# Loading a head pair's values onto partitions 32 to 95 in one transfer, and copying the overlaps and memory rows on chip

## Chip, cores, metric

One core of one Trainium2 chip. The metric is device time in microseconds (us). The record marks each run as fast or slow: of the seven runs of before beside runs 1 to 4, the fast ones took 338.6 to 340.5 us and the slow ones 343.93 to 348.09. The medians and ranges below are of all runs, a few slow ones among them; the ratios are of fast runs alone. PE is TensorE, DVE is VectorE, ACT is ScalarE, POOL is GpSimd, SPq is SyncE's queue, which issues most of the loads.

## The reference

Attention in chunks of 32 queries, each with 16 keys to its left, 8 to its right and 8 memory keys; then a Fourier mix over sequence and features, a layer norm and an MLP.

```python
batch, n_heads, seq, head_dim = (4, 8, 768, 64);  n_mem = 8
chunk, left_ctx, right_ctx = (32, 16, 8)
for c in range(seq // chunk):
    k_full = concat([mem_k, k[:, :, max(0, c0 - 16):min(S, c1 + 8)]])     # v_full alike
    a = softmax(scale * q_c @ k_full.T)
    out[:, :, c0:c1] = a @ v_full
x = out as (batch, seq, 512)
u = x + real(fft(fft(x, axis=1), axis=2))
return u + relu(layernorm(u) @ w_ch1) @ w_ch2        # w_ch1: 512 x 2048
```

## The kernel before

Work is cut into 16 head pairs (four per batch). Two chunks of 32 queries share one block of 64 sequence positions, so a block's products need 64 + 16 + 8 value rows and 8 memory rows on 128 partitions. All instructions are put in one fixed order per engine by a small planner (`Plan`), which uses costs written beside each task; on the chip every engine then goes through its list in order (in both traces PE and ACT pass from one line of the kernel to the next in the order of the list: PE 179 times before and 181 in the changed kernel, ACT 126 and 135).

```python
va = [spool.tile([P, NB, 66], FP32) for i in range(6)]           # one per head, two per pair

def e_load_v(n, hh):                                             # three loads per head
    nc.sync.dma_start(v1[16:64, 0:NT, 0:D], ...)                 # 48 rows
    nc.sync.dma_start(v1[0:16, 1:NB, 0:D], ...)                  # the 16 before them
    nc.sync.dma_start(v1[64:72, 0:NT, 0:D], mem_v[...].to_broadcast([NMEM, NT, D]))

def e_overlap(n, hh):                                            # the rows after the block
    nc.gpsimd.tensor_copy(v1[96:128, 0:NT, 0:D + 1], v1[0:32, 1:NB, 0:D + 1])

def e_kT(n):                                                     # keys, blocks 96 apart
    nc.scalar.copy(strided(kTb[n % NKT], 0, [[BS, NB], [8, 8], [1, RB]]), ...)

# ... cut: queries and keys are loaded (2 KB rows), cast (DVE in the first batch, POOL later),
#     turned on PE, copied by ACT; scores on PE, exponentials on ACT; then
def e_values(n, g):        # 24 products xa <- e1, va on PE; needs loads and overlaps
def e_norm(n, g):          # DVE: divides by the sum, writes xsb
# fourier(b): a chain of DVE steps zy, pq, ff, lo (two inputs in SBUF each) with ACT and PE between
# mlp(b): PE products ph and pc, ACT relu; they fill PE wherever it has nothing else
```

The softmax here doesn't subtract the row's maximum and nothing guards it: scores larger than these inputs give would overflow.

Of the kernel before, what the change touches and what calls it, by code (L numbers as in the profile page):

```python
# [16 lines left out]
CHUNK = 32  # L17
# [3 lines left out]
BIGM = 800.0  # L21

# [89 lines left out]
def kernel(  # L112
# [23 lines left out]
    NB = KP // 8  # L136
    BS = 96
# [18 lines left out]
    NV = 6  # L156
    va = [spool.tile([P, NB, 66], FP32, name=f"va{i}") for i in range(NV)]
    NKT = 2
    kTb = [spool.tile([P, NB * BS], BF16, name=f"kTb{i}") for i in range(NKT)]
# [4 lines left out]
    plan = Plan(dict(qf=NS, kf=NS, va=NV // 2, kTb=NKT, qb=1, kb=1, qT=2, tr=1, sc=1, xa=1, e1=3,  # L164
# [6 lines left out]
    mkf = cpool.tile([P, 2, D], FP32)  # L171
    mkb = cpool.tile([P, 2 * D], BF16)
# [11 lines left out]
    ident = cpool.tile([P, P], FP32)  # L184
# [25 lines left out]
    def e_masks():  # L210
        nc.gpsimd.memset(mbias, NEG)
        nc.gpsimd.memset(mbias[0:72, :], 0.0)
        nc.gpsimd.memset(mbias[96:128, 1:2], 0.0)
        nc.gpsimd.affine_select(out=mbias[0:64, 0:1], in_=mbias[0:64, 0:1],
                                compare_op=ALU.is_ge, fill=NEG,
                                base=CHUNK + LEFT + RIGHT - 1, pattern=[[0, 1]],
                                channel_multiplier=-1)
        nc.gpsimd.memset(mbias[0:32, 1:2], NEG)
        nc.gpsimd.affine_select(out=mbias[96:128, 1:2], in_=mbias[96:128, 1:2],
                                compare_op=ALU.is_ge, fill=NEG, base=RIGHT + LEFT - 1,  # L220
                                pattern=[[0, 1]], channel_multiplier=-1)
# [5 lines left out]
    def e_clear_act(t):  # L227
        flat = t if len(t.shape) == 2 else t.rearrange("p a b -> p (a b)")
        nc.scalar.copy(flat, zero[0:flat.shape[0]].to_broadcast(list(flat.shape)))

    def e_ones(i):
        nc.vector.memset(va[i][0:72, :, 64:65], 1.0)
        nc.vector.memset(va[i][0:16, 0, 64:65], 0.0)
        nc.vector.memset(va[i][0:64, NB - 1, 64:65], 0.0)
        nc.vector.memset(va[i][0:16, NB - 1, 64:65], 1.0)

# [12 lines left out]
    def e_load_k(n):  # L249
        b, pr = seq[n]  # L250
        nc.sync.dma_start(kf[n % NS][2:2 + QP],
                          k[b, 2 * pr:2 * pr + 2].rearrange("h (p j) d -> p h (j d)", j=RB))

    def e_load_v(n, hh):
        b, pr = seq[n]
        v1 = va[(2 * n + hh) % NV]
        vb = v[b, 2 * pr + hh]
        nc.sync.dma_start(v1[16:64, 0:NT, 0:D],
                          bass.AP(tensor=vb.tensor, offset=vb.offset,
                                  ap=[[D, 48], [64 * D, NT], [1, D]]))  # L260
        nc.sync.dma_start(v1[0:16, 1:NB, 0:D],  # L261
                          bass.AP(tensor=vb.tensor, offset=vb.offset + 48 * D,
                                  ap=[[D, 16], [64 * D, NT], [1, D]]))
        nc.sync.dma_start(v1[64:72, 0:NT, 0:D],
                          mem_v[b, 2 * pr + hh].unsqueeze(1).to_broadcast([NMEM, NT, D]))

# [13 lines left out]
    def e_overlap(n, hh):  # L280
        v1 = va[(2 * n + hh) % NV]
        nc.gpsimd.tensor_copy(v1[96:128, 0:NT, 0:D + 1], v1[0:32, 1:NB, 0:D + 1])  # L282

# [23 lines left out]
    def e_mkT(n):  # L307
        b, pr = seq[n]
        nc.vector.tensor_copy(
            kTb[n % NKT].rearrange("p (b c) -> p b c", b=NB)[:, 0:NT, 64:72],  # L310
            mkT[:, b * HP + pr, :].unsqueeze(1).to_broadcast([P, NT, NMEM]))

    def e_kT(n):
        nc.scalar.copy(  # L314
            strided(kTb[n % NKT], 0, [[BS, NB], [8, 8], [1, RB]]),
            strided(tr_of.pop((n, 1)), 0, [[8, NB], [1, 8], [KP, RB]]))
# [470 lines left out]
```

## Time and profile before

| | before |
|---|---|
| time, median of the first 3 runs | 342.63 us (341.51 to 344.22) |
| span of the profiled run | 339.3 us |
| busy: PE, DVE, ACT, POOL | 289.6, 183.2, 168.9, 80.6 us |
| 256-byte packets per pair: values, memory rows | 1536, 192 |
| loads per pair | 8 |

How to read it: PE is the engine to keep fed. Its idle time is almost all before 229 us, in the attention and Fourier parts of the four batches; the MLP of the first batch fills holes there, the other three follow it. So the question of any change is what it does to the end of the first batch's MLP: what comes after that takes some 155 to 158 us in every run below. The lines of the profile stand in the prediction.

### The profile page before, as it was taken

Reading aid. Unit: us, or ns where it says so; the run is one execution under the profiler, and the core shown is the slowest. Engines: PE = TensorE matmul, PEld = TensorE weight load, DVE = VectorE, ACT = ScalarE, POOL = GpSimd, SP = SyncE. Lnnn points to the kernel's source line nnn. Section 1 sums busy time; section 2 is a strip of 40 time slices with the busy share of each in tenths; the row PEclk is TensorE's granted clock in tenths of the full one; section 3 lists DMA queues with packets and bytes.
Section 4 is the critical chain, followed back from the end, with each engine's and each line's share of the span. In section 5 each row is a group of like instructions: output and inputs, shape, how many; then the busy total and the mean of one; then the engine's idle time right before and its main releaser. Section 6 shows DMA issues by size and latency. Waiting matters only on the chain.

```text
span 339.3 us, 6789 instructions
## 1 busy us (share of the span) xinstructions
PE 289.6 (85%) x2761; PEld 185.4 (55%) x2761; DVE 183.2 (54%) x356; ACT 168.9 (50%) x297; POOL 80.6 (24%) x89
## 2 busy tenths in 40 slices
PE   0678647969998886969999997898999999999995
PEld 0467536847565565547755654574445454554542
DVE  6964498868089899599773469782010100101001
ACT  7554885557637448676633623335436053250620
POOL 5634594224342637252001200000010000000000
PEclk9999999879999999898999999599999999999999
DMA  7999999999407785692063100000340100201001
GB/s 157 214 183 162 168 229 203 220 173 178 72 3 152 131 182 136 183 201 36 0 110 101 31 3 2 31 31 33 68 119 2 62 31 2 93 0 64 31 32 63
DMA packets 51839, 33.02 MB, mean 97 GB/s; under 512 B 40032, under 2 KB 42080, under 8 KB 51808
## 3 DMA queue, kind: packets, MB, share of 16 engines
q1 hardware_dynamic: 45376, 22.03, 36.9%
q0 software_dynamic: 2688, 4.19, 6.7%
q10 hardware_dynamic: 3744, 6.36, 4.9%
q8 instruction: 22, 0.36, 0.5%
q14 instruction: 9, 0.07, 0.1%
HBM read 28.11 MB, written 6.29 MB: 101 GB/s over the span
## 4 chain that ended last, share of the span: by engine, by line
PE 62%; DVE 14%; DMA 9%; ACT 4%; POOL 3%; issue 3%; SPq 3%; ACTq 0%; POOLq 0%
PE ph L496 23%; PE pc L510 22%; DMA qf<-in_q_dram 8%; PE xa L349 7%; PE pm L445 4%; PE ps L413 2%; SPq L261 2%; DVE zy L373 2%; DVE lo L403 2%; PE sc L325 1%; DVE ff L390 1%; DVE st L457 1%; DVE pq L381 1%; ACT e L333 1%; DVE pq L380 1%
## 5 line engine op out<-in xcount | busy, mean ns | idle before, releaser
L503 ACT ACTIVATE hT<-ph 128x384 f16<-128x384 f32 x128 | 61.2, 492 | 70.5 <-PE ph L496 70.3
L496 PE MATMUL ph<-unT,w_sb 128*128 128x384 f16 x512 | 92.2, 327 | 2.4 <-ACT hT L503 1.8
L510 PE MATMUL pc<-w_sb,hT 128*128 128x512 f16 x384 | 87.3, 382 | 0.0
L516 DVE SCALAR_TENSOR_TENSOR osb<-pc,rstd,xsb 128x512 f32<-128x512 f32 x24 | 17.8, 746 | 98.3 <-PE pc L510 98.3
L496 PEld LDWEIGHTS <-w_sb 128*128 128x128 f16 x512 | 48.3, 97 | 37.9 <-issue 8.2
L510 PEld LDWEIGHTS <-hT 128*128 128x128 f16 x384 | 37.2, 98 | 42.4 <-issue 1.5
L282 POOL COPY va<-va 32x780 f32<-32x780 f32 x32 | 36.2, 1138 | 50.0 <-DMA va<-in_v_dram 37.9
L333 ACT ACTIVATE e<-sc,mbias 128x384 f32<-128x384 f32 x64 | 33.7, 579 | 20.0 <-PE sc L325 19.1
L349 PE MATMUL xa<-va,e 128*64 128x65 f32 x768 | 35.4, 253 | 8.6 <-ACT e L333 3.7
L349 PEld LDWEIGHTS xa<-va,e 128*64 128x64 f32 x768 | 30.6, 162 | 15.7 <-issue 7.7
L463 ACT ACTIVATE un<-xsb,mu_s 128x512 f16<-128x512 f32 x24 | 17.3, 722 | 24.5 <-DVE mu_s L458 15.8
L359 DVE RECIPROCAL zs<-xa 128x6 f32<-128x6 f32 x32 | 6.1, 190 | 34.5 <-PE xa L349 34.3
L325 PE MATMUL sc<-qT,kTb 64*128 64x64 bf16 x384 | 12.8, 207 | 12.6 <-ACT kTb L314 11.0
L484 POOL TENSOR_SCALAR rstd<-mu_s 128x6 f32<-128x6 f32 x4 | 1.0, 244 | 89.7 <-DVE osb L516 83.7
L413 PE MATMUL ps<-cosS,lo 128*128 128x193 f16 (+1 forms) x72 | 16.6, 285 | 4.6 <-DVE lo L403 4.5
L274 POOL CAST qb<-qf 96x1024 bf16<-96x1024 f32 x12 | 14.9, 1242 | 20.8 <-DMA qf<-in_q_dram 11.9
L413 PE MATMUL ps<-cosS,hi 128*128 128x193 f16 (+1 forms) x72 | 16.7, 285 | 3.4 <-DVE ff L390 3.2
L425 ACT CAST up<-ps 128x386 f16<-128x386 f32 x16 | 9.7, 605 | 19.4 <-PE ps L413 17.8
L325 PEld LDWEIGHTS <-kTb 64*128 64x128 bf16 x384 | 8.8, 104 | 18.5 <-ACT kTb L314 12.3
L360 DVE TENSOR_TENSOR xsb<-xa,zs 128x384 f32<-128x384 f32 x32 | 17.8, 557 | 1.1
L398 ACT CAST hi<-ff 128x768 f16<-128x768 f32 x16 | 13.2, 832 | 10.1 <-DVE ff L390 9.9
L403 DVE TENSOR_TENSOR lo<-ff,hi 128x768 f16<-128x768 f32 x16 | 16.8, 1063 | 2.2 <-ACT hi L398 2.1
(90 smaller groups left out, 356.2 us busy)
## 6 DMA issues: line engine op xcount, KB each, us to landing
qf<-in_q_dram SPq DMA_DIRECT2D x16, 384.0 KB
kf<-in_k_dram SPq DMA_DIRECT2D x16, 384.0 KB
out_dram<-osb ACTq DMA_DIRECT2D x24, 256.0 KB, 2.0
va<-in_v_dram SPq DMA_DIRECT2D x32, 144.0 KB, 5.8
w_sb<-in_moe_w_ch_dram POOLq DMA_DIRECT2D x8, 512.0 KB, 16.1
va<-in_v_dram SPq DMA_DIRECT2D x32, 48.0 KB, 6.8
va<-in_mem_v_dram SPq DMA_DIRECT2D x32, 24.0 KB
unT<-un SPq DMA_TRANSPOSE x18, 2.4
```

The costliest lines, as they stand in the source:

```text
L282: nc.gpsimd.tensor_copy(v1[96:128, 0:NT, 0:D + 1], v1[0:32, 1:NB, 0:D + 1])
L325: nc.tensor.matmul(sc[:, hh, t6, :], kT[r0:r0 + 64, t * BS:t * BS + P], qT[r0:r0 + 64, ts(t, 64)], start=True, stop=True, tile_position=(r ...
L333: nc.scalar.activation(e1[:, :, :, ts(half, 32)], sc[:, :, 0:6, ts(half, 32)], AFT.Exp, bias=mbias[:, half:half + 1], scale=1.0 / math.sqr ...
L349: nc.tensor.matmul(xa[64 * half:64 * half + 64, st, hh, 0:65], e1[:, hh, t6, :], v1[:, 6 * g + t6, 0:65], start=True, stop=True)
L360: nc.vector.tensor_tensor(xs[b][:, 3 * g:3 * g + 3, 2 * pr * D:(2 * pr + 2) * D] .rearrange("p s (h d) -> p s h d", h=2), xa[:, :, :, 0:D] ...
L403: nc.vector.tensor_tensor(lo[:, ab].rearrange(fl), ff_of[b, par][:, ab].rearrange(fl), hi[:, ab].rearrange(fl), ALU.subtract)
L413: nc.tensor.matmul(out_[:, sp, :], part[:, ab, sp * 3 + st, c0:c1], tab[:, sp, st, :], start=(st == 0 and i == 0), stop=(st == 2 and i == 1))
L463: nc.scalar.activation(un, xs[b][:, kt, :], AFT.Identity, bias=mu_of[b][:, kt, 0:1], scale=-1.0)
L496: nc.tensor.matmul(ph[:, 0:384], w1_sb[:, dt, ts(ht, P)], unT_of[b][:, dt, sh * 384:(sh + 1) * 384], start=(dt == 0), stop=(dt == NDT - 1))
L503: nc.scalar.activation(hT_of[b, sh][:, ht, :], ph_of.pop((b, sh, ht))[:, 0:384], AFT.Relu, bias=0.0, scale=-1.0)
L510: nc.tensor.matmul(pc_of[b, sh, stl], hT_of[b, sh][:, ht, ts(stl, P)], w2_sb[:, ht, :], start=(ht == 0), stop=(ht == NHT - 1))
L516: nc.vector.scalar_tensor_tensor(osb, pc_of.pop((b, sh, stl)), rstd_of[b][:, st:st + 1], xs[b][:, st, :], ALU.mult, ALU.add)
```

## The change

Intent: the value loads are many 256-byte packets to few partitions. Bring the 64 rows of a block onto partitions 32 to 95 in one transfer for both heads, and make the rest (left overlap, right overlap, twelve-fold memory rows) by copies on chip, so that fewer loads and packets are needed. Cut to its core:

```diff
-    va = [spool.tile([P, NB, 66], FP32, name=f"va{i}") for i in range(6)]
+    va = [spool.tile([P, 2, NT, 66], FP32, name=f"va{i}") for i in range(3)]
+    mv = [spool.tile([NMEM, 2, D], FP32, name=f"mv{i}") for i in range(3)]
-    kTb = [spool.tile([P, NB * BS], BF16, name=f"kTb{i}") for i in range(NKT)]
+    kTb = [spool.tile([P, NT, P], BF16, name=f"kTb{i}") for i in range(NKT)]
@@ loads: six per pair become two
+        nc.sync.dma_start(mv[n % NV], mem_v[b, 2 * pr:2 * pr + 2].rearrange("h m d -> m h d"))
+        nc.sync.dma_start(v1[PAD:PAD + 64].rearrange("p h t c -> p (h t) c")[:, :, 0:D],
+                          vb.rearrange("h (t p) d -> p (h t) d", p=64))
@@ copies
-        nc.gpsimd.tensor_copy(v1[96:128, 0:NT, 0:D + 1], v1[0:32, 1:NB, 0:D + 1])     # per head
+        if side == 0:                                                              # per pair
+            nc.gpsimd.tensor_copy(v1[0:32, :, 1:NT, 0:D + 1], v1[64:96, :, 0:NT - 1, 0:D + 1])
+        else:
+            nc.gpsimd.tensor_copy(v1[96:128, :, 0:NT - 1, 0:D + 1], v1[32:64, :, 1:NT, 0:D + 1])
+    def e_memv(n, eng):                            # DVE in the first batch, POOL in the others
+        eng.tensor_copy(va[n % NV][0:NMEM, :, :, 0:D],
+                        mv[n % NV].unsqueeze(2).to_broadcast([NMEM, 2, NT, D]))
@@ keys: 13 groups of 8 instead of 8, blocks 128 apart
-            strided(kTb[n % NKT], 0, [[BS, NB], [8, 8], [1, RB]]),
+            strided(kTb[n % NKT], PAD - 8 * KOFF, [[P, NT], [8, 13], [1, RB]]),
@@ planner's costs
-        lv = [add("SP", 1.1, ..., moved=2.3) for hh in range(2)]
+        lv = add("SP", 0.8, lambda: e_load_v(n), ..., take=("va",), moved=2.0)
-        ov = [add("POOL", 0.84, lambda hh=hh: e_overlap(n, hh), [lv[hh]]) for hh in range(2)]
+        ov = [add("POOL", 1.55, lambda side=side: e_overlap(n, side), [lv]) for side in range(2)]
+        ov.append(add(cn, 1.0 if first else 1.7, lambda: e_memv(n, ce), [ov[0]]))
```

Left out: the masks for the new places, cleared and set buffers, three constants moved into other buffers.

More of the change, by code (lines that the diff above doesn't have):

```diff
@@ L21 @@
 BIGM = 800.0
+PAD = 32
+KOFF = 3
 def rev_ap(src, last, count, outer=()):
@@ L135 @@
     KP = QP + 8
-    NB = KP // 8
-    BS = 96
     HS = S // 2
@@ L155 @@
     kf = [spool.tile([KP, 2, RB * D], FP32, name=f"kf{i}") for i in range(NS)]
-    NV = 6
-    va = [spool.tile([P, NB, 66], FP32, name=f"va{i}") for i in range(NV)]
+    NV = 3
+    va = [spool.tile([P, 2, NT, 66], FP32, name=f"va{i}") for i in range(NV)]
+    mv = [spool.tile([NMEM, 2, D], FP32, name=f"mv{i}") for i in range(NV)]
     NKT = 2
-    kTb = [spool.tile([P, NB * BS], BF16, name=f"kTb{i}") for i in range(NKT)]
+    kTb = [spool.tile([P, NT, P], BF16, name=f"kTb{i}") for i in range(NKT)]
     HP = H // 2
     seq = [(b, pr) for b in range(B) for pr in (0, 2, 1, 3)]
-    plan = Plan(dict(qf=NS, kf=NS, va=NV // 2, kTb=NKT, qb=1, kb=1, qT=2, tr=1, sc=1, xa=1, e1=3,
+    plan = Plan(dict(qf=NS, kf=NS, va=NV, kTb=NKT, qb=1, kb=1, qT=2, tr=1, sc=1, xa=1, e1=3,
                      xsb=3, fold=2, hl=1, up=4, dn=4, acc=2, mlp=2, un=3, unT=2, hT=1, osb=3))
@@ L170 @@
     NPR = B * H // 2
-    mkf = cpool.tile([P, 2, D], FP32)
-    mkb = cpool.tile([P, 2 * D], BF16)
+    mkf = fpool.tile([P, 2, D], FP32, tag="osb", bufs=3, name="mkf")
+    mkb = fpool.tile([P, 2 * D], BF16, tag="osb", bufs=3, name="mkb")
     mkT = cpool.tile([P, NPR, NMEM], BF16)
@@ L183 @@
     zero = cpool.tile([P, 1], FP32)
-    ident = cpool.tile([P, P], FP32)
+    ident = fpool.tile([P, P], FP32, tag="osb", bufs=3, name="ident")
     ident_h = cpool.tile([P, P], FP16)
@@ L210, in e_masks @@
     def e_masks():
-        nc.gpsimd.memset(mbias, NEG)
-        nc.gpsimd.memset(mbias[0:72, :], 0.0)
-        nc.gpsimd.memset(mbias[96:128, 1:2], 0.0)
-        nc.gpsimd.affine_select(out=mbias[0:64, 0:1], in_=mbias[0:64, 0:1],
-                                compare_op=ALU.is_ge, fill=NEG,
-                                base=CHUNK + LEFT + RIGHT - 1, pattern=[[0, 1]],
-                                channel_multiplier=-1)
-        nc.gpsimd.memset(mbias[0:32, 1:2], NEG)
-        nc.gpsimd.affine_select(out=mbias[96:128, 1:2], in_=mbias[96:128, 1:2],
-                                compare_op=ALU.is_ge, fill=NEG, base=RIGHT + LEFT - 1,
-                                pattern=[[0, 1]], channel_multiplier=-1)
+        nc.gpsimd.memset(mbias, 0.0)
+        for half in range(2):
+            first, last = PAD - LEFT + CHUNK * half, PAD + CHUNK * (half + 1) + RIGHT - 1
+            nc.gpsimd.affine_select(out=mbias[:, half:half + 1], in_=mbias[:, half:half + 1],
+                                    compare_op=ALU.is_ge, fill=NEG, base=last,
+                                    pattern=[[0, 1]], channel_multiplier=-1)
+            nc.gpsimd.affine_select(out=mbias[:, half:half + 1], in_=mbias[:, half:half + 1],
+                                    compare_op=ALU.is_ge, fill=NEG, base=-first,
+                                    pattern=[[0, 1]], channel_multiplier=1)
+        nc.gpsimd.memset(mbias[0:NMEM, :], 0.0)
     def e_scales():
@@ L227, in e_clear_act @@
     def e_clear_act(t):
-        flat = t if len(t.shape) == 2 else t.rearrange("p a b -> p (a b)")
+        flat = t.rearrange("p a b -> p (a b)" if len(t.shape) == 3 else "p a b c -> p (a b c)")
         nc.scalar.copy(flat, zero[0:flat.shape[0]].to_broadcast(list(flat.shape)))
     def e_ones(i):
-        nc.vector.memset(va[i][0:72, :, 64:65], 1.0)
-        nc.vector.memset(va[i][0:16, 0, 64:65], 0.0)
-        nc.vector.memset(va[i][0:64, NB - 1, 64:65], 0.0)
-        nc.vector.memset(va[i][0:16, NB - 1, 64:65], 1.0)
+        nc.vector.memset(va[i][0:NMEM, :, :, D:D + 1], 1.0)
+        nc.vector.memset(va[i][32:64, :, :, D:D + 1], 1.0)
+        nc.vector.memset(va[i][64:96, :, :, D:D + 1], 1.0)
     def e_mkf():
@@ L250, in e_load_k, with e_load_v @@
         b, pr = seq[n]
-        nc.sync.dma_start(kf[n % NS][2:2 + QP],
+        nc.sync.dma_start(kf[n % NS][KOFF:KOFF + QP],
                           k[b, 2 * pr:2 * pr + 2].rearrange("h (p j) d -> p h (j d)", j=RB))
-    def e_load_v(n, hh):
+    def e_load_v(n):
         b, pr = seq[n]
-        v1 = va[(2 * n + hh) % NV]
-        vb = v[b, 2 * pr + hh]
-        nc.sync.dma_start(v1[16:64, 0:NT, 0:D],
-                          bass.AP(tensor=vb.tensor, offset=vb.offset,
-                                  ap=[[D, 48], [64 * D, NT], [1, D]]))
-        nc.sync.dma_start(v1[0:16, 1:NB, 0:D],
-                          bass.AP(tensor=vb.tensor, offset=vb.offset + 48 * D,
-                                  ap=[[D, 16], [64 * D, NT], [1, D]]))
-        nc.sync.dma_start(v1[64:72, 0:NT, 0:D],
-                          mem_v[b, 2 * pr + hh].unsqueeze(1).to_broadcast([NMEM, NT, D]))
+        v1 = va[n % NV]
+        vb = v[b, 2 * pr:2 * pr + 2]
+        nc.sync.dma_start(mv[n % NV], mem_v[b, 2 * pr:2 * pr + 2].rearrange("h m d -> m h d"))
+        nc.sync.dma_start(v1[PAD:PAD + 64].rearrange("p h t c -> p (h t) c")[:, :, 0:D],
+                          vb.rearrange("h (t p) d -> p (h t) d", p=64))
     qT_of, kT_of, qb_of, kb_of, tr_of, e1_of, sc_of, xa_of, xs = ({} for _ in range(9))
@@ L278, in e_cast_k, with e_overlap @@
         eng.tensor_copy(kb_of[n].rearrange(cp_b), kf[n % NS].rearrange(cp_q, j=RB))
-    def e_overlap(n, hh):
-        v1 = va[(2 * n + hh) % NV]
-        nc.gpsimd.tensor_copy(v1[96:128, 0:NT, 0:D + 1], v1[0:32, 1:NB, 0:D + 1])
+    def e_overlap(n, side):
+        v1 = va[n % NV]
+        if side == 0:
[5 more added lines that the diff above has]
+                        mv[n % NV].unsqueeze(2).to_broadcast([NMEM, 2, NT, D]))
     def e_turn_q(n):
@@ L309, in e_mkT @@
         nc.vector.tensor_copy(
-            kTb[n % NKT].rearrange("p (b c) -> p b c", b=NB)[:, 0:NT, 64:72],
+            kTb[n % NKT][:, :, 0:NMEM],
             mkT[:, b * HP + pr, :].unsqueeze(1).to_broadcast([P, NT, NMEM]))
@@ L314, in e_kT @@
         nc.scalar.copy(
-            strided(kTb[n % NKT], 0, [[BS, NB], [8, 8], [1, RB]]),
-            strided(tr_of.pop((n, 1)), 0, [[8, NB], [1, 8], [KP, RB]]))
+            strided(kTb[n % NKT], PAD - 8 * KOFF, [[P, NT], [8, 13], [1, RB]]),
+            strided(tr_of.pop((n, 1)), 0, [[8, NT], [1, 13], [KP, RB]]))
     def e_scores(n, g):
@@ L324, in e_scores @@
                 r0 = 64 * hh
-                nc.tensor.matmul(sc[:, hh, t6, :], kT[r0:r0 + 64, t * BS:t * BS + P],
+                nc.tensor.matmul(sc[:, hh, t6, :], kT[r0:r0 + 64, t, :],
                                  qT[r0:r0 + 64, ts(t, 64)], start=True, stop=True,
@@ L345, in e_values @@
             for hh in range(2):
-                v1 = va[(2 * n + hh) % NV]
+                v1 = va[n % NV]
                 for half in range(2):
@@ L349, in e_values @@
                     nc.tensor.matmul(xa[64 * half:64 * half + 64, st, hh, 0:65],
-                                     e1[:, hh, t6, :], v1[:, 6 * g + t6, 0:65],
+                                     e1[:, hh, t6, :], v1[:, hh, 6 * g + t6, 0:65],
                                      start=True, stop=True)
@@ L528 @@
     t_id = add("POOL", 0.5, lambda: make_identity(nc, ident))
-    t_clear["va", 0] = add("ACT", 1.0, lambda: e_clear_act(va[0]), [t_zero])
-    t_clear["va", 1] = add("POOL", 0.9, lambda: nc.gpsimd.memset(va[1], 0.0))
+    t_clear["va", 0] = add("ACT", 1.8, lambda: e_clear_act(va[0]), [t_zero])
     t_scales = add("DVE", 0.2, e_scales, [t_iota])
@@ L535 @@
         t_clear["kf", i] = add("ACT", 1.15, lambda i=i: e_clear_act(kf[i]), [t_zero])
-        for m in (2 * i, 2 * i + 1):
-            t_clear["va", m] = add("ACT", 1.0, lambda m=m: e_clear_act(va[m]), [t_zero])
+        t_clear["va", i] = add("ACT", 1.8, lambda i=i: e_clear_act(va[i]), [t_zero])
     for i in range(NKT):
@@ L572, in attention @@
                  take=("kf",), moved=1.3)
-        lv = [add("SP", 1.1, lambda hh=hh: e_load_v(n, hh),
-                  [t_ones[2 * n + hh] if 2 * n < NV else None],
-                  take=("va",) if hh == 0 else (), moved=2.3) for hh in range(2)]
+        lv = add("SP", 0.8, lambda: e_load_v(n), [t_ones[n] if n < NV else None],
+                 take=("va",), moved=2.0)
         first = b == 0
@@ L586, in attention @@
                  take=("kTb",))
-        ek = add("ACT", 0.85, lambda: e_kT(n), [tk, mk], give=(ktag,))
+        ek = add("ACT", 1.15, lambda: e_kT(n), [tk, mk], give=(ktag,))
         for g in range(2):
```

## The prediction

> **What bounds the kernel now.** I read the page first (busy shares and slices), then busy time by stretches of 10 us, then the chain of work that ended last, the waits (those of the transfer queue too), the groups, and last the transfer packets that the trace records.
>
> ```profile
> PE 289.6 (85%) x2761; PEld 185.4 (55%) x2761; DVE 183.2 (54%) x356; ACT 168.9 (50%) x297; POOL 80.6 (24%) x89
> PE   0678647969998886969999997898999999999995
> DVE  6964498868089899599773469782010100101001
> DMA  7999999999407785692063100000340100201001
> ```
>
> TensorE works 289.6 of 339.3 us; 49.7 us are idle. From 229 us on it does nothing but the two MLP products and is full: no change to the loads can shorten that. The transfers are full in the first nine slices, about 76 us, and then loosen.
>
> ```profile
> 40.00:50.00 10.00, 2.77 (x30) 2.30 (x31) 9.86 (x20) 8.77 (x14) 9.84 (x11) 1.00 1.12 205
> 70.00:80.00 10.00, 7.28 (x88) 5.61 (x89) 6.71 (x18) 5.09 (x10) 2.07 (x2) 0.83 1.09 166
> 90.00:100.00 10.00, 10.00 (x113) 5.71 (x111) 5.44 (x7) 4.67 (x8) 3.74 (x3) 1.00 0.01 2
> 110.00:120.00 10.00, 6.91 (x88) 4.68 (x88) 8.55 (x13) 5.11 (x8) 6.75 (x6) 1.00 0.81 133
> 140.00:150.00 10.00, 7.71 (x113) 4.91 (x112) 8.89 (x14) 7.82 (x15) 3.94 (x5) 1.00 1.00 178
> ```
>
> The columns are the stretch, then busy us of PE, weight loads, DVE, ACT, POOL, then clock, transfer share and GB/s. From all such rows the idle time of PE is: 0 to 40 us 15.9; 40 to 80 us 12.5; 80 to 100 us 0.2; 100 to 160 us 11.0; 160 to 210 us 0.9; after that 9.9, of which some 5 are the tail. From 90 to 100 us nothing is loaded at all.
>
> ```profile
> 32.79 7.19 DMA qf<-in_q_dram
> 40.10 1.03 POOL qb L274
> ...
> 48.45 7.04 SPq L261
> ...
> 57.05 14.37 DMA qf<-in_q_dram
> 71.54 1.04 POOL qb L274
> 72.63 0.66 PE trq L288 x8
> ...
> 100.89 3.01 DMA out_dram<-osb
> 104.28 0.34 SPq L264
> 104.71 4.47 DMA qf<-in_q_dram
> ```
>
> The chain runs through the loads three times: query loads that stand 7 and 14 us in full queues, and at 104 us the loading queue, which has just waited for a store of the output. Head pairs of the second batch are thus finished late: their last value products start at 92.1 and 94.3 us, and the second batch's Fourier work on DVE begins only then (zy at 96 us). DVE is busy 9.8 of 20 us from 80 to 100 us: waiting, not bound.
>
> ```profile
> SPq L261 <- DMA out_dram<-osb: 20.0, 2, 19.5
> SPq L251 <- DMA kf<-in_k_dram: 7.4, 8, 1.1
> ```
>
> The second line, with the landing times in the trace, shows a rule of this program: a load starts only when the load issued eight earlier on it has landed (35.97 then 36.05 us, 43.21 then 43.27, 75.62 then 75.64). A pair has eight loads, so about one pair is on its way at a time. The first line is the same rule caught on an output store: 19.5 us without a load, just before 104 us.
>
> [...] 256-byte packets take 18 ns while the first pair is alone (some 360 land per 0.5 us), but 38 to 50 ns later, and then 170 to 260 land per 0.5 us. [...] the POOL overlap copy takes 827 ns at best and 1138 on average, DVE's small kTb copy 174 at best and 391 on average. [...] 24 value products take 1.57 us before 45 us and 0.85 later.
>
> **The change, part by part.**
>
> ```profile
> L282 POOL COPY va<-va 32x780 f32<-32x780 f32 x32 | 36.2, 1138 | 50.0 <-DMA va<-in_v_dram 37.9
> L274 POOL CAST qb<-qf 96x1024 bf16<-96x1024 f32 x12 | 14.9, 1242 | 20.8 <-DMA qf<-in_q_dram 11.9
> L314 ACT COPY kTb<-trk 128x832 bf16<-128x832 bf16 x16 | 13.7, 854 | 5.6 <-PE trk L304 4.6 <-POOL va L282 0.9
> ```
>
> Loads. A pair moves 384 packets of 2 KB (query, key), 1536 of 256 B (values) and 192 of 256 B (memory rows, twelve-fold); after it, 384, 1536 and 16. While full, pairs follow each other every 7 us (query landings near 8.5, 15, 21.5, 29.5). The 2 KB packets land at about 65 per 0.5 us: 384 / 65 x 0.5 = 2.95 us. The rest, about 4 us, is values. If all value packets run as in the undisturbed stretch, 1536 / 360 x 0.5 = 2.1 us. Estimate after: 2.95 + 2.1 + 0.3 = 5.4 us per pair, 1.6 less; eight pairs are loaded in the full stretch, so 13 us of transfer time go. With four loads per pair the rule of eight spans two pairs, so the 19.5 us wait is likely to shrink or go.
>
> POOL. The overlap is two copies of 32 x (2 x 11 x 65 = 1430) instead of two of 32 x 780: 834 ns (the median) x 1430 / 780 = 1.53 us alone, x 1138 / 834 = 2.09 us disturbed. The memory copy (8 x 1536) at 1.07 ns per element is 1.64 us, disturbed as the cast is (1242 / 1033) 1.97 us. A pair of batches two to four costs 2 x 2.09 + 1.97 + 1.24 + 1.08 = 8.5 us on POOL, now 2 x 1.14 + 2.32 = 4.6. In all 80.6 + 32 x 0.95 + 12 x 1.97 - 0.8 = 134 us. Twelve pairs need 102 us of the 165 between 33 and 198 us: it lies beside other work, but a batch takes 34 us and can't follow faster.
>
> ACT. The key copy grows from 832 to 1248 elements. From 800 ns at 768 and 854 at 832 the slope is 0.84 ns: 1.2 us, 16 x 0.35 = 5.6 us more; in the first batch it lies on the chain (11.0 and 19.2 us), so about 1 us there.
>
> DVE. Four memory copies in the first batch: the 1024-element cast takes 0.68, so 1.0 us each, 4 us, in a batch where DVE still makes tables; perhaps 0.5 us on the path. Summed over minimum, locks cost DVE some 20 us now; POOL's extra 53 us of a present 80 might add 10, and perhaps 2 on the path, since its Fourier chain is broken by other waits.
>
> PE does the same products. The score product's keys begin at 128-element steps instead of 96, which should change nothing. The moved constants and smaller count of memsets are worth less than 1 us.
>
> **Where it lands.** The first batch (to 38 us) [...] about 6.5 us per pair; faster loads don't help, and the first pair's overlap takes two longer copies: +1.5 us with the key copy. From 40 to 80 us the wait for the query at 71.5 us (2.8 us of idle PE) should go, and about 1 of the 50 to 60 us stretch: -3.5. The second batch's attention should end near 76 us, limited by POOL, instead of 95, so DVE starts its Fourier part up to 19 us sooner, and TensorE still has the first MLP (42 us) to fill with. Of 11.0 us of idle from 100 to 160 us I take 7 back. With it the last 3.6 us hole (210 to 220 us) shrinks by 1 to 2. Locks and longer POOL latency give 2 back. Sum: 1.5 - 3.5 - 7 - 1.5 + 2 = -8.5, and I take another 2 for work of the last pair that moves into idle time before 80 us: -10.5 us, 342.6 to 332.
>
> **Rivals.** A: the loads shrink but TensorE hides it: idle before 160 us is of DVE's making (DVE is 8.6 to 10 busy in most of 100 to 160 us), so only the 3.5 us come back and the first batch costs 1.5: about 340. For it: after 95 us the chain is full of DVE. Against it: DVE was half idle just before. B: POOL becomes the pace. At 8.5 us per pair, overlaps come after the point that the fixed order of the other engines assumes, and TensorE, in order, stands before value products; PE would lose 5 to 10 us, time 340 to 350. For it: POOL work on copies grows by half as much again as all POOL does now. Against it: it had 76% idle. C: everything falls into place and PE is full from 77 us on: 240 us of work left, less 3.5 done earlier, plus 8 of holes and tail: span 322, time 325.
>
> **Range and chances.** My sum sits between C (one in four) and A (three in ten), with B one in ten. So 332, range 323 to 341. Two per cent is 335.8: faster 0.6, within 0.34, slower 0.06.
>
> **What would show it.** Right: about four loads per pair, value packets at about 18 to 25 ns, transfers no longer full to 76 us, no PE wait for the query near 71 us, the second batch's last value products before 82 us, zy of it before 84 us, PE idle from 100 to 160 us under 6 us. Wrong: value packets still at 40 ns; value products or exponentials waiting for the overlap or memory copies; a new long wait of the load queue on an output store; DVE operations stretched by over 15 us in sum; POOL over 150 us.

## The result

358.78 us, median of 4 runs (354.18 to 359.25), against 342.59 of before (341.51 to 344.22): ratio 1.0438, 95% interval 1.0343 to 1.0534. The change is slower. (A ratio here and below is the mean time of one kernel's fast runs over that of the other's fast runs of the same rounds, so not the ratio of the medians quoted. The two differ most in runs 1 to 4: four of the seven runs of before in that job were slow, its median is 343.93, its fast runs took 338.6 to 340.5.)

The page of the changed kernel, busy time and slices as shown of before:

```profile
PE 291.1 (81%) x2761; PEld 185.5 (52%) x2761; DVE 215.9 (60%) x345; ACT 173.7 (49%) x295; POOL 127.1 (36%) x100
PE   1556836689928588947899999598999999999995
DVE  6999299898799969799883357978010010201001
DMA  6982899943935009790004310010051010100101
```

PE does the same work (291.1 us) in a longer span: some 17 us more are idle. The transfers are no longer full throughout the first 76 us (two of the first eight slices are well below, six are still at 8 or 9 tenths). The packets themselves are faster, as foreseen: those of a pair's values took 18 to 25 ns on average in the first 36 us, where before they took 23 in the first pair and 37 to 44 in those after it, and up to 570 of them landed per 0.5 us (292 GB/s; a pair's 1536 value packets landed in 1.72 us, 228 GB/s). But DVE is busy 32.7 us longer, and 47 us more went to POOL. Stretches of 10 us; the columns are PE, weight loads, DVE, ACT, POOL, clock, transfer share, GB/s:

```profile
100.00:110.00 10.00, 3.07 (x35) 2.51 (x34) 9.93 (x9) 4.11 (x6) 9.76 (x7) 0.71 0.16 38
120.00:130.00 10.00, 4.94 (x31) 3.06 (x29) 9.08 (x11) 3.04 (x4) 5.41 (x3) 0.74 0.01 2
160.00:170.00 10.00, 6.72 (x40) 4.71 (x39) 10.00 (x10) 4.63 (x8) 7.53 (x4) 0.54 0.23 41
```

In these DVE is full, PE is a third to two thirds busy, and little is loaded. In the first row DVE gets through nine instructions in 10 us. Four of DVE's instructions there, with three of POOL's, from the instructions in order of time (start, length, both in us):

```profile
97.50 1.67 DVE L380 TENSOR_TENSOR pq<-zy 128x768 f32<-128x768 f32 x1
98.43 1.98 POOL L276 COPY va<-va 32x1430 f32<-32x1430 f32 x1
99.10 2.12 DVE L381 TENSOR_TENSOR pq<-zy 128x768 f32<-128x768 f32 x1
100.47 1.99 POOL L278 COPY va<-va 32x1430 f32<-32x1430 f32 x1
101.26 1.24 DVE L389 COPY ff<-pq 128x6 f32<-128x6 f32 x1
...
102.52 2.14 POOL L281 COPY va<-mv 8x1536 f32<-8x1536 f32 x1
103.26 2.42 DVE L389 COPY ff<-pq 128x6 f32<-128x6 f32 x1
```

The two engines take turns. The `pq` at 97.50 waits until POOL's cast ends (98.36) and then runs its own 0.8 us or so; POOL's copy at 98.43 waits until that `pq` ends (99.17) and then runs its own 1.2 us; the next `pq` waits for it, and so on. (Each is some 0.13 us shorter than alone, 0.81 against 0.95 and 1.24 against 1.37; records of neighbours on one engine overlap here by up to 0.11 us.) A `pq` alone takes 0.95 us, the copy of six elements 0.15: here 2.12 and 2.42. That last copy ends (105.68) only when two of POOL's instructions have ended, the copy at 102.52 (104.66) and a cast after it (105.65). By groups (count, then busy us and mean ns of one), first two of before, then the changed kernel:

```profile
L373 DVE TENSOR_TENSOR zy<-xsb 128x768 f32<-128x768 f32 x16 | 16.3, 1021 | 0.2
L403 DVE TENSOR_TENSOR lo<-ff,hi 128x768 f16<-128x768 f32 x16 | 16.8, 1063 | 2.2 <-ACT hi L398 2.1
```

```profile
L276 POOL COPY va<-va 32x1430 f32<-32x1430 f32 x16 | 31.2, 1952 | 23.5 <-DMA va<-in_v_dram 14.3
L281 POOL COPY va<-mv 8x1536 f32<-8x1536 f32 x12 | 22.0, 1833 | 0.6
L373 DVE TENSOR_TENSOR zy<-xsb 128x768 f32<-128x768 f32 x16 | 24.1, 1515 | 0.2
L403 DVE TENSOR_TENSOR lo<-ff,hi 128x768 f16<-128x768 f32 x16 | 21.9, 1374 | 0.1
L314 ACT COPY kTb<-trk 128x1248 bf16<-128x1248 bf16 x16 | 19.2, 1202 | 0.8 <-PE trk L304 0.8
```

I call the **stretch** of DVE the sum, over all its instructions in the trace, of the time above the shortest of the same line and operation. It was 21.4 us before and is 51.4 now. (The prediction's "locks" are this sum. Records of neighbours overlap a little, so it is a measure, not a share of the span. It does not put the runs below in their order: run 15 has 41.0 and is slower than the changed kernel.)

Where on the way it was lost, in us from the start, from the first and last instruction of each part in the traces:

| | before | changed |
|---|---|---|
| first batch's values done | 39.9 | 44.4 |
| first batch's Fourier part done (last `st`) | 80.7 | 82.3 |
| first product of the MLP | 76.6 | 80.7 |
| second batch's values done | 95.2 | 94.2 |
| second batch's Fourier part, length from second `zy` to last `st` | 35.4 | 46.5 |
| third batch's, likewise | 32.7 | 38.5 |
| fourth batch's (POOL has nothing to copy then) | 30.7 | 30.3 |
| first batch's MLP done | 181.4 | 199.8 |
| end | 339.3 | 357.4 |

All 18 us are lost before the first batch's MLP is done, and the two Fourier parts that run beside POOL's copies are 11.1 and 5.8 us longer, the one that doesn't is not.

### The profile page after: what moved, and what is told of

Same layout as the page of the kernel before. It is cut to its first block, busy times and chain, and to the rows that moved or that the text cites. A ratio compares the mean times of both kernels' runs of the same rounds, so it can differ in the third digit from the quotient of the medians.

```text
span 357.4 us, 6684 instructions
## 1 busy us (share of the span) xinstructions
PE 291.1 (81%) x2761; PEld 185.5 (52%) x2761; DVE 215.9 (60%) x345; ACT 173.7 (49%) x295; POOL 127.1 (36%) x100
## 4 chain that ended last, share of the span: by engine, by line
PE 60%; DVE 31%; ACT 5%; issue 3%; ACTq 0%; DVEq 0%
PE ph L496 22%; PE pc L510 22%; PE xa L349 6%; PE ps L413 5%; DVE zy L373 4%; PE pm L445 4%; DVE lo L403 3%; DVE ff L390 3%; DVE pq L381 3%; DVE pq L380 2%; DVE st L457 2%; DVE ff L389 2%; DVE xsb L451 2%; ACT e L333 1%; DVE va L281 1%
## 5 line engine op out<-in xcount | busy, mean ns | idle before, releaser
L276 POOL COPY va<-va 32x1430 f32<-32x1430 f32 x16 | 31.2, 1952 | 23.5 <-DMA va<-in_v_dram 14.3
L278 POOL COPY va<-va 32x1430 f32<-32x1430 f32 x16 | 26.9, 1679 | 0.9
L373 DVE TENSOR_TENSOR zy<-xsb 128x768 f32<-128x768 f32 x16 | 24.1, 1515 | 0.2
L398 ACT CAST hi<-ff 128x768 f16<-128x768 f32 x16 | 13.4, 837 | 20.0 <-DVE ff L390 19.8
L281 POOL COPY va<-mv 8x1536 f32<-8x1536 f32 x12 | 22.0, 1833 | 0.6
L403 DVE TENSOR_TENSOR lo<-ff,hi 128x768 f16<-128x768 f32 x16 | 21.9, 1374 | 0.1
L413 PE MATMUL ps<-cosS,hi 128*128 128x193 f16 (+1 forms) x72 | 17.8, 298 | 4.8 <-DVE ff L390 3.2
L413 PE MATMUL ps<-cosS,lo 128*128 128x193 f16 (+1 forms) x72 | 17.6, 297 | 4.5 <-DVE lo L403 4.5
L413 PEld LDWEIGHTS <-lo 128*128 128x128 f16 (+1 forms) x120 | 13.8, 115 | 11.9 <-DVE lo L403 11.1
L314 ACT COPY kTb<-trk 128x1248 bf16<-128x1248 bf16 x16 | 19.2, 1202 | 0.8 <-PE trk L304 0.8
## 6 DMA issues: line engine op xcount, KB each, us to landing
w_sb<-in_moe_w_ch_dram POOLq DMA_DIRECT2D x8, 512.0 KB, 14.3
```

The source lines that it names most:

```text
L276: nc.gpsimd.tensor_copy(v1[0:32, :, 1:NT, 0:D + 1], v1[64:96, :, 0:NT - 1, 0:D + 1])
L278: nc.gpsimd.tensor_copy(v1[96:128, :, 0:NT - 1, 0:D + 1], v1[32:64, :, 1:NT, 0:D + 1])
L281: eng.tensor_copy(va[n % NV][0:NMEM, :, :, 0:D], mv[n % NV].unsqueeze(2).to_broadcast([NMEM, 2, NT, D]))
L314: nc.scalar.copy(strided(kTb[n % NKT], PAD - 8 * KOFF, [[P, NT], [8, 13], [1, RB]]), strided(tr_of.pop((n, 1)), 0, [[8, NT], [1, 13], [KP, ...
L373: nc.vector.tensor_tensor(zy_of[b, par][:, :, c0:c0 + P], xb[:, :, c0:c0 + P], xb[:, :, HD + c0:HD + c0 + P], ALU.add if par == 0 else ALU ...
L403: nc.vector.tensor_tensor(lo[:, ab].rearrange(fl), ff_of[b, par][:, ab].rearrange(fl), hi[:, ab].rearrange(fl), ALU.subtract)
```

## The experiments

Three theories. **P**: POOL's reading copies and DVE's operations with two inputs in SBUF exclude each other, and the longer copies stretch the Fourier chain. **O**: the new costs gave the planner a worse order. **L**: POOL's sheer length makes values late. For the gain that did not come there is also **D**: the faster loads were hidden anyway. (The "rival D" in the expectations of 2, 8 and 13 is another: small transfers fill the queues again.) I write "before" for the median of that kernel in the same job.

### 1. POOL writes as long, but reads nothing

```diff
-            nc.gpsimd.tensor_copy(v1[0:32, :, 1:NT, 0:D + 1], v1[64:96, :, 0:NT - 1, 0:D + 1])
+            nc.gpsimd.memset(v1[64:96, :, 1:NT, 0:D + 1], 0.001)
-            nc.gpsimd.tensor_copy(v1[96:128, :, 0:NT - 1, 0:D + 1], v1[32:64, :, 1:NT, 0:D + 1])
+            nc.gpsimd.memset(v1[32:64, :, 1:NT, 0:D + 1], 0.001)
@@ memory rows on POOL
+            eng.memset(va[n % NV][0:NMEM, :, :, 0:D], 0.001)
```

> The changed kernel with its POOL copies (both overlaps, the memory rows of batches two to four) replaced by memsets of the same shapes on POOL, in the same places and the same order; wrong results on purpose. POOL then works as long as before on va (about 1.4 us each) but reads nothing. Theory P (POOL's reads and DVE's two-input operations exclude each other): DVE's stretching (time over each group's minimum, summed) falls from 51 us to 25 or less, and the time from 358.8 to 345 or less. Rival O (the fixed order, computed with the new costs, is worse) and rival L (POOL's sheer length makes the values late): DVE may shorten, but the time stays above 352.

Measured: 341.48 us (338.41 to 343.97), before 343.93, ratio 1.0081 (0.991 to 1.0253). The result is wrong on purpose. The stretch is 29.2 us, above the 25 that I had set. The same places and waits in the order, and 17 us are gone against the 358.78 of the changed kernel (another job; the fast runs, 338.4 to 343.2 and 354.2 to 359.3, don't touch). Two things in the edit besides: the memsets write the copies' source rows, so most values are one constant, and a constant exponent (`mhalf`) was changed with them. Run 6 below has random data.

```profile
L276 POOL MEMSET va<- 32x1430 f32 x16 | 22.5, 1409 | 30.8 <-DMA va<-in_v_dram 25.7 <-PE ph L499 4.6
L278 POOL MEMSET va<- 32x1430 f32 x16 | 21.8, 1365 | 0.7
L384 DVE TENSOR_TENSOR pq<-zy 128x768 f32<-128x768 f32 x8 | 7.6, 950 | 0.0
L312 DVE COPY kTb<-mkT 128x96 bf16<-128x96 bf16 x16 | 8.3, 519 | 0.4 <-PE sc L328 0.3
```

The memsets are stretched little (1409 and 1365 ns on average, 1282 at best, 3.3 us in all; the copies in their places 1952 and 1679, 1367 at best, 14.3 us in all), and `pq` is back at 950 ns on average. The small one-input copy into `kTb` still takes 519 ns, 177 at best. So P holds, with a remainder: POOL is 22 us less busy than in the changed kernel, and 341 is not the 332 of run 5, which has no copies.

### 2. All rows by transfer

```diff
-        nc.sync.dma_start(mv[n % NV], mem_v[...])
+        # per head: v1[16:32, hh, 1:NT], v1[96:104, hh, 0:NT-1] from v, v1[0:8, hh, :] from mem_v
     (no overlap and no memory copies; the planner's costs as in the changed kernel)
```

> The changed kernel with both overlaps and the memory rows loaded again by transfers (six small ones per pair beside the large one onto partitions 32 to 95), no copy on chip, order unchanged. Theory P: DVE's stretching falls to about 15 us, below the kernel before (21), and the time to 335 to 343. Rival O: above 352. Rival D (the transfers were the point: 720 more packets of 256 B per pair fill them again): transfers full to 76 us again, 345 or more.

Measured: 348.03 us (345.22 to 351.37), before 343.93, ratio 1.0222 (1.004 to 1.0404); the result is right. Stretch 12.4 us, as theory P asked, but the time did not follow all the way, as rival D said: the transfers are full again, a pair now takes nine loads, and the first batch's values end at 50.5 us. It is still 11 us faster than the changed kernel; the small transfers cost 16 against run 5, which has neither them nor copies.

### 3. The kernel before in the order of the change

```diff
-        lv = [add("SP", 1.1, ..., moved=2.3) for hh in range(2)]
+        lv = add("SP", 0.8, lambda: (e_load_v(n, 0), e_load_v(n, 1)), ..., moved=2.0)
-        ov = [add("POOL", 0.84, ...
+        ov = [add("POOL", 1.55, ...
+        ov.append(add(cn, 1.0 if first else 1.7, lambda: None, [ov[0]]))
```

> The kernel before, its instructions unchanged, but ordered by the costs that the change gives its planner (values of a pair as one task, memory copy as a task that issues nothing). Rival O: 350 or more. Theory P: the order matters little, 338 to 347.

Measured: 342.52 us (339.27 to 343.68), before 343.93, ratio 1.0072 (0.9945 to 1.0199). The new costs alone do no harm to the kernel before. And runs 1 and 5 keep the changed kernel's own order and take 341 and 332 us, so theory O falls for this change. (How much order can weigh in this kernel otherwise, see 14.)

### 4 and 6. The kernel before with as much more POOL work

```diff
         nc.gpsimd.tensor_copy(v1[96:128, 0:NT, 0:D + 1], v1[0:32, 1:NB, 0:D + 1])
+        for _ in range(3 if hh == 1 and n >= HP else 1):
+            nc.gpsimd.tensor_copy(v1[96:128, 0:NT, 0:D + 1], v1[0:32, 1:NB, 0:D + 1])   # 4
+            nc.gpsimd.memset(v1[96:128, 0:NT, 0:D + 1], 0.001)                          # 6 instead
```

> The kernel before with its overlap copy done twice per head, and four times for the second head of each pair of batches two to four: 56 more copies of 834 ns, 47 us of POOL work, as the change adds; nothing else changed, the result stays right. Theory P: DVE's stretching rises from 21 to 40 us or more and the time to 349 or more. Rival O: under 345.

> As the run with 56 more POOL copies in the kernel before (353 us), but the 56 added instructions are memsets of the same shape on the same rows, which write and don't read; wrong results on purpose. Theory P (reads exclude DVE's two-input operations): most of the 10 us go, 342 to 347. If POOL's sheer time, or its writes, make the loss: 350 or more.

Measured: with copies 353.33 us (352.97 to 355.76), before 343.93, ratio 1.0421 (1.0327 to 1.0515), result right. With memsets 342.18 us (339.52 to 344.18), before 344.0, ratio 0.9986 (0.9886 to 1.0086), wrong on purpose. The added instructions, first with copies, then with memsets:

```profile
L284 POOL COPY va<-va 32x780 f32<-32x780 f32 x56 | 58.7, 1048 | 3.5
151.69 4.45 POOL L284 COPY va<-va 32x780 f32<-32x780 f32 x3
153.87 1.58 DVE L383 TENSOR_TENSOR pq<-zy 128x768 f32<-128x768 f32 x1
```

```profile
L284 POOL MEMSET va<- 32x780 f32 x56 | 43.2, 771 | 3.3
142.85 2.35 POOL L284 MEMSET va<- 32x780 f32 x3
143.53 0.95 DVE L383 TENSOR_TENSOR pq<-zy 128x768 f32<-128x768 f32 x1
```

The last two lines of each are three added instructions in a row, with a `pq` that starts while they run: beside copies both are stretched, beside memsets neither. It is so throughout the two traces (counted where one had at least 0.3 us left when the other began). Of `zy`, `pq`, `ff` and `lo` with two inputs, 13 began while a POOL copy ran, and all 13 were lengthened by about the rest of that copy; 22 copies began while one of them ran, and all 22 were lengthened likewise. With memsets, 3 and 15 met in this way: none was lengthened by more than 17 ns. In run 1, with memsets too, 13 of 15 and 8 of 8 went unhindered; the other two waited on into a cast that followed the memset. DVE's small one-input copies did wait for memsets (4 of 5 here, 8 of 8 in run 1).

43 us of memsets between the overlap and the value products that wait for them cost nothing; copies in the same places cost the 4% that the change cost. That is P against L (a memset is a little shorter, 742 ns against 829 at best, 5 us in all), in a kernel with none of the change's other parts. The stretch rose only to 30.5 us with copies (I had said 40) and to 26.9 with memsets: it is a rough guide, and the time moved by more than it. Part of the loss with copies is thus probably the same lock on its other side: POOL's own lengthening (20.5 us with copies, 7.7 with memsets, over the shortest of each), which makes values late. I did not part the two.

### 5. No copies at all

```diff
     def e_overlap(n, side): ...
+        return
     def e_memv(n, eng): ...
+        return
```

> The changed kernel with neither the overlap copies nor the memory copies, all else in its place and order; wrong results on purpose (overlap and memory rows stay zero). It is the most that the faster loads could give. If my prediction's sum for the loads (-12 us) was right and only the copies spoiled it: 325 to 333. If the loads were hidden (rival A of the prediction): 337 to 343.

Measured: 332.12 us (330.08 to 332.38), before 344.0, ratio 0.9677 (0.959 to 0.9764); wrong on purpose, the data stay random. The first batch's values end at 41.7 us, its Fourier part at 75.6, the second's at 122.0, the first MLP at 174.1. So the copies on chip cost 27 us (359 against 332): 80 us of POOL's time (127.1 busy against 46.9), and four copies on DVE. The 12 us below the kernel before are not the loads' alone, as that kernel has 36 us of overlap copies, which are gone here too. Run 13 below has no copies either, and transfers at least as full as before, and is 6 us below before already: some 5 us are left for the faster loads, no more than two plans can differ by. D is not refuted.

### 7. Memory rows by transfer

```diff
+            nc.sync.dma_start(v1[0:NMEM, hh, :, 0:D], mem_v[...].to_broadcast([NMEM, NT, D]))
     def e_memv(n, eng): ...
+        return
```

> The changed kernel with its memory rows loaded twelve-fold by two transfers per pair again, the overlap copies kept on POOL, order unchanged. By POOL time the memory copies are 22 of the 47 us that POOL gained, and the 4 on DVE go too; if the loss of 16 us goes by time: 349 to 353. Rival: the loss comes from the overlaps of the first batch and the long copies, 354 or more.

Measured: 352.05 us (350.05 to 352.78), before 344.0, ratio 1.027 (1.0191 to 1.0348). The result was wrong, and that was not meant: the left overlap's copy writes partitions 0 to 31 and comes after the load, so it covers the memory rows. The overlap copies are the same, so I let the time stand: without the memory copies 7 us of the loss are gone, less what the two loads cost, and the larger rest is left with the overlaps.

### 8, 11 and 12. Left overlap by transfer, and who copies the rest

```diff
+            nc.sync.dma_start(v1[16:32, hh, 1:NT, 0:D], ...)          # 8, 11, 12: left overlap
+            nc.sync.dma_start(v1[0:8, hh, :, 0:D], mem_v[...])        # 8, 12: memory rows
-        ov = [... e_overlap(n, side) for side in range(2)]
+        ov = [add("POOL", 1.7, lambda: e_overlap(n, 1), [lv])]        # 12: "ACT", 1.4
+        # 11: e_memv on ACT
```

> A candidate: the large transfer onto partitions 32 to 95, the left overlap (16 rows) and the memory rows by small transfers, only the right overlap copied on POOL (one copy of 1.5 us per pair, less than the 1.67 of before), planned anew with these costs. Theory P: DVE's stretching at 20 us or less; [...] 334 to 342. Rival D (the small transfers fill the queues again): 343 to 350.

> Candidate: large transfer, left overlap by two small transfers per pair, right overlap on POOL (1.5 us per pair), memory rows on ACT. Beside the candidate with memory rows loaded (341.5) it has 192 packets of 256 B less per pair and 23 us more on ACT: 335 to 341.

> Candidate: as the one with left overlap and memory rows loaded (341.5 us), but the right overlap copied by ACT, so POOL copies nothing of va. Theory P: DVE's stretching falls from 24 us to 15 or less and the time to 333 to 339. Rival (its transfers are the bound): 340 or more.

Measured, all with right results: 341.53 us (339.34 to 342.05), ratio 0.996 (0.9883 to 1.0036); 364.77 us (363.1 to 365.6), ratio 1.0682 (1.0584 to 1.0781); 349.09 us (347.66 to 350.32), ratio 1.0214 (1.0128 to 1.03). The first came out at the edge of what was foreseen, level with before (stretch 23.7 us, not 20). The two with ACT missed my figures by 24 and 10 us or more. In 12 the stretch did fall, to 13.9 us, and the time rose all the same: 22 us of copies on ACT cost 8 us more than the same copies on POOL in 8. In 11 the memory rows' copies on ACT cost 23 us more than their transfers in 8, at about the same stretch (25.1 us). So there are losses in this kernel that a stretched DVE does not explain; each of these runs has its own plan too.

### 9 and 10. Copies on ACT

```diff
-            nc.gpsimd.tensor_copy(v1[0:32, ...
+            nc.scalar.copy(v1[0:32, ...                               # 9: both overlaps
-        eng.tensor_copy(va[n % NV][0:NMEM, ...
+        nc.scalar.copy(va[n % NV][0:NMEM, ...                         # 9 and 10: memory rows
```

> The changed kernel with all three copies (both overlaps, memory rows) on ACT, planned anew; the result stays right. ACT takes an estimated 1.35 us for 1430 elements and 1.45 for 1536 (slope 0.84 ns per element, from its copies of 768 and 832), 16 x 4.15 = 66 us more on an engine busy 174. [...] it lands near the run without copies (332): 332 to 340. Rival: ACT becomes the pace of the attention (about 8.5 us per pair), 343 or more.

> The changed kernel with the memory rows alone copied by ACT (16 x 1.45 us), overlaps on POOL; the result stays right. It repeats, with a right result, the run that loaded them (352): 346 to 353. If the memory copies were most of the loss: under 343.

Measured, both right: 382.36 us (377.92 to 383.64), ratio 1.1146 (1.1007 to 1.1284), and 368.84 us (367.44 to 371.86), ratio 1.0805 (1.07 to 1.091). For the first the rival holds: DVE's stretch is down to 14.2 us, but ACT is busy 240.7 us (173.7) and value products wait for exponentials (54.2 us in all, 29 times). The 332 to 340 supposed that what DVE and POOL wait for each other is the whole loss. For the second, the waits of the profile show (second and third line) two of the ways in which one slow engine stops another:

```profile
POOL va L276 <- DMA va<-in_v_dram: 36.7, 11, 11.9
ACT va L281 <- POOL va L276: 7.8, 2, 7.3
PE sc L325 <- ACT kTb L314: 10.0, 1, 10.0
```

ACT's memory copy stands in its list behind POOL's overlap, and what ACT does next (keys, exponentials) waits with it. Why it comes to 369, I did not follow to the end.

### 13, 14 and 16. Overlaps inside the large transfer, no copy

A transfer of 96 partitions (8 to 103) per head brings a block's rows and both overlaps at once for ten of twelve blocks; the first and last block, which have no neighbour, come in two small ones.

```diff
+        for hh in range(2):
+            nc.sync.dma_start(v1[8:104, hh, 1:NT - 1, 0:D],
+                              bass.AP(..., offset=vb.offset + (hh * S + 64 + 8 - PAD) * D,
+                                      ap=[[D, 96], [64 * D, NT - 2], [1, D]]))
+        for t, lo, hi in ((0, 32, 112), (NT - 1, 16, 96)):
+            nc.sync.dma_start(v1[lo:hi, :, t, 0:D], ...)
+        # memory rows: two loads; no e_overlap, no e_memv
+        lv = add("SP", 2.3, ..., moved=3.4)        # 14: moved=4.6; 16: SP 1.8, moved=2.6
```

> The changed layout without any copy on chip: per head one transfer of 96 partitions (8 to 103) brings values and both overlaps of ten blocks, two small ones bring the first and last block of both heads, two the memory rows; eight loads per pair, [...] Right result. If copies were the loss and transfers suffice: 333 to 340. Rival D (as with all rows by small transfers, 348): 343 or more.

> The same instructions, planned with a transfer cost of 4.6 us per pair for the values instead of 3.4 (the kernel before used 4.6). Order theory: within 3 us of the run beside it.

> Same instructions as the right-result run at 336.7 us, planned with a transfer cost of 2.6 us and less issue time. If nearness of the planned cost to the real one [...] is what counts: 337 to 343. If a more hopeful plan is always better, as the other plans of the changed kernel were hopeful: under 336.

Measured, all right: 336.71 us (334.03 to 339.87), before 342.36, ratio 0.982 (0.9722 to 0.9917); 344.22 us (342.03 to 346.07), ratio 1.0063 (0.9993 to 1.0133); 338.53 us (336.69 to 343.41), before 342.93, ratio 0.9893 (0.9823 to 0.9963), over five rounds. The first is a version that, with this plan, beats both kernels, by about 2% and 6%. The page of its profile:

```profile
PE 283.9 (85%) x2761; PEld 180.9 (54%) x2761; DVE 174.3 (52%) x347; ACT 173.6 (52%) x295; POOL 46.7 (14%) x56
DMA  6999999999999297960145000100520100101001
```

Its transfers are full for its first 13 slices, some 108 us, longer than before, and it is faster all the same: DVE's stretch is 11.0 us and POOL has only the casts. The three differ in nothing but the plan, and by up to 7.5 us. My expectation that the order would be worth 3 us at most was wrong; the plan with the middle cost (3.4 us, against 2.6 and 4.6) was the best of three, which is no proof of a trend. (What a pair's values really took in run 13 was my estimate, not measured.) Differences of 2% in this kernel must be read with that in mind; the change's 4.4% and the 27 us between 5 and the changed kernel, which share one plan, are beyond it.

### 15. The first batch's memory copies on POOL

```diff
-        ov.append(add(cn, 1.0 if first else 1.7, lambda: e_memv(n, ce), [ov[0]]))
+        ov.append(add("POOL", 1.7, lambda: e_memv(n, nc.gpsimd), [ov[0]]))
```

> The changed kernel with the memory copies of the first batch on POOL, like the others, instead of DVE. If DVE's four copies and its waiting for POOL's overlap cost the first batch its 4.4 us: 353 to 356, first batch's values done by 42 us. If POOL is the narrower place there: 358 or more.

Measured: 363.09 us (361.15 to 363.55), before 342.36, ratio 1.0598 (1.0533 to 1.0664); the first batch's values end at 48.4 us instead of 44.4. DVE was the better place of the two. The loss of the first batch is not those four copies: run 7, which loads the memory rows instead, ends it at 44.5. Without any copy it ends at 41.7.

## Why the prediction was wrong

The step that failed is "Locks and longer POOL latency give 2 back", and with it "POOL's extra 53 us of a present 80 might add 10, and perhaps 2 on the path, since its Fourier chain is broken by other waits". The stretch grew by 30 us, not 10, and the copies cost not 2 us on the path but 27 against no copies at all (run 5) and 17 against memsets in their places (run 1), all in one plan. Against the copies that the kernel before has, the nearest measure is run 4: as much POOL work added to that kernel cost 4.2%, some 14 us. The other steps in turn:

- **Loads**: right about the transfers. Values landed at 18 to 29 ns per packet (the means of a pair, to 112 us), the loads of a pair halved and the long wait of the load queue on an output store (19.5 us) went. Whether the new partitions or less other traffic made the packets faster, no run shows. Nor was the rule of eight varied: in the trace of before, 7 of the 8 loads to 76 us for which the landing of the load issued eight earlier is recorded began within 0.08 us of it, which may come from the program as built. (The "38 to 50 ns" of before are 37 to 44 as means of a pair.) What they are worth is not shown: run 5's -12 us, the sum that I had foreseen, are for the loads and for the copies that before has (see there). Nor did they come in the way that I summed: I counted 12 us of PE's idle time back, and in its profile (330.6 us against 339.3) PE is idle 48.1 us against 49.7. It is busy 7.1 us less with the same products, spread over many groups (`ps` 29.9 to 28.0 us, `pc` 87.3 to 85.8, `xa` 35.4 to 34.3). Why, no run shows, and run 6 has PE busy only 282.2 us at the time of before. That my total without the locks' cost is close to its 332 is therefore luck in good part.
- **POOL**: the size was right (127.1 us busy, foreseen 134). The conclusion "it lies beside other work" was wrong. I asked whether POOL's hours suffice, which they do (run 6 has 119.9 us of it and loses nothing). I should have asked what DVE does in those hours: its chain `zy`, `pq`, `ff`, `lo` is made of operations with two SBUF inputs, exactly those that waited for POOL's copies in run 4, all 13 that met one.
- **Scaling the lock**: I scaled the stretch by POOL's time. But in the changed kernel POOL has copies standing ready, one after another (L278 waited for anything 0.9 us in all 16), and then one DVE instruction after another waits for a POOL instruction and the other way round. A 0.95 us step becomes 2.1 us and more. That they come one after another is the change's own doing: it makes three copies ready at the same time, and faster loads feed them (18 to 25 ns per packet, 37 to 44 before).
- **"Beside other waits"**: while heads were still being loaded, DVE was half idle only from 80 to 100 us. In the Fourier parts it was mostly at 8.6 to 10 of 10 us, in the rows that I showed myself, and PE's MLP filler didn't last over the longer chain: PE was idle 23.1 us between 80 and 200 us, where it was 11.9 before. I foresaw 7 us of it back from 100 to 160 us: there it was 18.5 us, after 11.0.
- **Second batch's attention near 76 us**: wrong even without copies (87.6 us in run 5, 94.2 in the changed kernel). The value products stand in PE's list between the Fourier products of the batch before, and PE ran its list in order (all 181 passages from line to line); SPq then waits for PE to free a buffer (97.2 us in all, 19.8 before). That this order is the reason is argued from the traces, not tested. Run 5 moved it by 8 us, not 19.
- **ACT**: right (the key copy 1202 ns, foreseen 1200). **First batch**: +1.5 foreseen, +4.5 measured, of which run 5 has 1.8.
- **Rival B** ("POOL becomes the pace") gave the right side and up to 350 us, and I gave it one in ten. Its way was not quite what happened either: PE waited less for POOL than for DVE, and DVE for POOL.
- **The clock column**: the 1.00 in the row of 40 to 50 us says nothing. That trace has no clock record before 52.4 us, and the value products at 38.4 us still took 1.57 us, as they did in the changed kernel from 36.4 to 50.7 us, where its trace records a clock of 0.50.

Left open: run 1 keeps 9 us over run 5. Four memory copies on DVE, the stretched one-input copies and POOL's remaining length are in it; I did not part them.

## What to carry to other kernels

Before moving work to an engine that looks idle, ask which of the busy engines will wait for it, and look at what that engine does in the same stretch: here DVE's operations with two SBUF inputs waited for POOL's copies (13 of 13 that met one in run 4; a `pq` of the changed kernel took 2.12 us for 0.95) and not for its memsets (none of 3 in run 6), and 80 us of copies on an engine that is otherwise busy for 47 of 330 us cost 27 us. A memset in place of a copy keeps the order and nearly the time (742 ns for 829, 1282 for 1367, at best), and takes the reads away; it tells this kind of loss from mere lateness in one run. And a transfer can place overlapping rows itself: in run 13 one transfer per head with overlapping source rows did what two of the three copies per pair did, and two small ones brought the memory rows, at the cost of 2432 packets of 256 B per pair instead of 1552.
